# Attention and two MLPs on one Trainium2 core: weight jobs in three steps an f tile apart, and other points for loads on the SP queue

## The chip, the cores and the metric

The kernel runs on one core of one Trainium2 chip. The metric is the device time of one execution in microseconds (us). The engines are TensorE (PE in the profile, PEld for its weight loads), VectorE (DVE), ScalarE (ACT), GpSimd (POOL) and SyncE (SP, which here only issues DMAs). SP, ScalarE and POOL each have an instruction stream of their own from which they issue DMAs in order.

## The reference

```
scores = q k^T / sqrt(64)            # (4, 8, 576, 64): batch, heads, positions, head size
# heads 0..3 see the last 32 positions, heads 4..7 every 32nd position before and at their own
attn   = softmax(where(mask, scores, -1e9)) v
x      = attn with heads side by side          # 2304 tokens x 512
x      = (s * relu(x w_in)^2 + b) w_out        # w_in 512 x 2048, w_out 2048 x 512
out    = ((x w_a) * (x w_b)) w_o               # w_a, w_b 512 x 1536, w_o 1536 x 512
```

All data are float32; the weights arrive as 64-bit floats, and each is turned into a float32 on the chip by integer operations.

## The kernel before

**Numbers as two words.** Every matmul operand is a pair of words: a high one that ScalarE copies into the matmul's type, and a low one that VectorE gets by subtraction. A product is three passes (high x high, high x low, low x high).

**First MLP (`h_mm`, `o_mm`).** Tokens come in five groups n = 0..4 of 512, 384, 512, 384 and 512. For each n there are 16 tiles f. `h_mm` makes 12 matmuls, then ScalarE applies ReLU (L795) into the one buffer `r`, squares it and makes the high word; VectorE makes the low word `gt` (L123 or L806). `o_mm` comes two tiles behind and adds 12 matmuls to four accumulating banks `acc`. The attention of group n + 1 and the conversion of the second MLP's weights run beside the tiles of n = 1, 2 and 3.

**Conversion (`convert_w2`, class `Stream`).** In 37 steps the generator loads 64-bit words (`raw`, two buffers; w_a, w_b, w_o of a tile in turn, kinds 0, 1, 2), converts those of the step before, and stores them to DRAM as `w2d`. For kind 2 it also splits words and stores them as `w2o` (L858). `Stream` calls it at most once an f tile: `due` grows by a rate, and a step takes 1 plus what it yields; kind 2 yields `MORE`. The load of w_b goes into the buffer that the split of w_o leaves.

**Weight jobs (`sums`, `work`).** The second MLP uses Strassen-like sums of weight quarters: s1, s2, s3, s4 from the plain words a11, a12, a21, a22. A job loads two plain tiles `w2r` (POOL, L876), makes the four sums in a tile `w2t` (VectorE, L887; two buffers), copies the high word into a `spare` room (ScalarE, L894), subtracts for the low word (VectorE, L897), and stores both (POOL, L902) to `w2s` or `w2o`. These are eight calls of a generator: load, four sums, high, low, stores. 16 jobs run in n = 4: `work(f + 1)` at tile f calls the load of the next job, then all the rest of its own. Two more run in pair 0 of the second MLP.

**Second MLP.** It has three pairs of 384-token blocks. For each pair, 12 tiles g multiply seven weight forms with seven forms of x, in the order a11, s2, s3, s1, a12, a22, s4, six matmuls each (`product`, tile `pp`): banks pa, pb and pd of a pool of three, and pc of a pool of one, are taken anew at each g. `fill("s2", i)` and `fill("s3", i)` load forms from `w2s`; `source` loads plain words into `wsrc` and `fill("a11", i)`, `fill("a22", i)` split them on ScalarE and VectorE. Both engines' work is in an order written out by `act` and `dve` (each instruction behind the last), and SP's loads by `queue_sp`. At g = 5 `x2_load` loads the x of the next pair (1.5 MB), `x2_bias` and `x2_forms` turn it into forms later. Then 42 products `o2_mm` make the output; `o2_load` loads their weights `o2w` (256 KB) into NW rooms in turn. `o2_post` and `send` add banks up and store the output in pieces of 32 columns.

**What sets the order.** Where no order is written, the framework's scheduler fixes each engine's order when the kernel is built, with times that it simulates; `after` and `in_order` add edges. A tile that takes a buffer waits for the last user of it.

## Time and profile before

| | us |
|---|---|
| median of 3 runs | 916.59 (916.41 to 917.19) |
| the profiled execution | 914.19 |
| its span, first to last instruction | 912.5 |
| TensorE matmul busy in the span | 881.8 (97%) |
| TensorE weight load busy | 807.7 (89%) |
| VectorE busy | 681.7 (75%) |
| ScalarE busy | 408.2 (45%) |
| POOL busy | 143.0 (16%) |

Times in the rows are microseconds from the span's start. n = 4 begins near 395 us, the second MLP's pair 0 near 492, its output products near 590. An engine executes in order, so an instruction that waits holds up all behind it. "Granted clock" is the share of TensorE's full clock of 2.4 GHz; the lower level is 0.5.

### The profile page before, as it was taken

What the parts mean: (1) busy time and instruction counts of PE and PEld (TensorE: products, weight loads), DVE (VectorE), ACT (ScalarE), POOL (GpSimd) and SP (SyncE); (2) the same over time, 40 slices, a digit from 0 to 9 for tenths busy, and PEclk for the clock granted to TensorE, in tenths of its full rate; (3) what the DMA queues carried; (4) which work ended last, traced back from release to release, by engine and by line L of the source; (5) the groups of instructions that cost most, each with busy time, mean ns of one, the idle gap of its engine ahead of it and who ended that gap; (6) DMA issues with size and microseconds to landing.
All of it is one profiled execution on the core that took longest, in us unless ns stands there. A gap on an engine that the chain in (4) does not pass through costs nothing.

```text
span 912.5 us, 17335 instructions
## 1 busy us (share of the span) xinstructions
PE 881.8 (97%) x6274; PEld 807.7 (89%) x6274; DVE 681.7 (75%) x1411; ACT 408.2 (45%) x878; POOL 143.0 (16%) x289
## 2 busy tenths in 40 slices
PE   8999999999999989999999899999999999999996
PEld 6778889998888879997878889999989999999995
DVE  6898986776776867737667668896867896786883
ACT  6777764444433343456555224263224273232350
POOL 6000000000110011114443101007100005100013
PEclk9999999999999999999999999999999999999999
DMA  9966535775865767458988786787675787666585
GB/s 229 293 190 167 160 76 138 179 192 150 237 193 158 180 197 189 142 165 294 319 293 311 268 305 220 255 271 227 208 254 175 258 270 220 210 202 200 160 270 154
DMA packets 184260, 195.69 MB, mean 214 GB/s; under 512 B 107856, under 2 KB 137296, under 8 KB 184176
## 3 DMA queue, kind: packets, MB, share of 16 engines
q1 hardware_dynamic: 165760, 146.98, 54.9%
q0 software_dynamic: 15536, 46.90, 14.7%
q10 hardware_dynamic: 2880, 0.72, 0.4%
q8 instruction: 49, 0.80, 0.4%
q14 instruction: 35, 0.29, 0.1%
HBM read 152.08 MB, written 42.47 MB: 213 GB/s over the span
## 4 chain that ended last, share of the span: by engine, by line
PE 56%; DMA 13%; issue 13%; DVE 7%; ACT 5%; POOL 4%; SPq 2%; POOLq 0%; DVEq 0%; ACTq 0%
PE pp L99 24%; PE o L99 12%; PE h L99 8%; PE acc L99 7%; DMA wsrc<-w2d 3%; DMA w2d<-w2s 1%; DMA w2s<-w2t 1%; DMA raw<-in_moe_w_b_dram 1%; DMA o2w<-w2o 1%; POOL w2s L902 1%; DMA wf<-w2s 1%; SPq L284 1%; POOL w2r L876 1%; ACT raw L141 1%; PE po L99 1%
## 5 line engine op out<-in xcount | busy, mean ns | idle before, releaser
L99 PE MATMUL pp<-x2w,wf 128*128 128x384 f32 x1296 | 235.3, 338 | 8.1 <-DVE u L618 4.6
L99 PEld LDWEIGHTS pp<-x2w,wf 128*128 128x128 f32 x1296 | 228.1, 190 | 10.0 <-DVE u L618 5.2
L99 PE MATMUL h<-x,w 128*128 128x512 f32 (+1 forms) x960 | 219.0, 376 | 2.6 <-ACT r L795 2.2
L99 PE MATMUL acc<-gt,w 128*128 128x512 f32 (+2 forms) x960 | 211.4, 369 | 1.1 <-ACT w L122 1.0
L99 PEld LDWEIGHTS acc<-gt,w 128*128 128x128 f32 x960 | 175.9, 188 | 24.6 <-ACT w L122 1.4
L99 PEld LDWEIGHTS h<-x,w 128*128 128x128 f32 x960 | 172.6, 189 | 28.2 <-ACT r L795 3.3
L99 PE MATMUL o<-gf,o2w 128*128 128x384 f32 x756 | 133.4, 337 | 2.4 <-DMA o2w<-w2o 2.4
L99 PEld LDWEIGHTS o<-gf,o2w 128*128 128x128 f32 x756 | 131.3, 188 | 4.1 <-DMA o2w<-w2o 2.6
L613 ACT ACTIVATE gf<-quad 128x384 fp32r<-128x384 f32 x126 | 64.9, 524 | 94.3 <-DVE quad L618 64.9
L1276 POOL DMA_DIRECT2D out_dram<-ot x93 | 52.2, 570 | 295.9 <-DVE ot L1262 285.4
L795 ACT ACTIVATE r<-h 128x512 f32<-128x512 f32 (+1 forms) x80 | 44.4, 555 | 118.8 <-PE h L99 90.4
L618 DVE TENSOR_TENSOR gf<-quad,gf 128x384 fp32r<-128x384 f32 x126 | 67.5, 554 | 7.1 <-ACT gf L613 5.1
L618 DVE TENSOR_TENSOR quad<-pp,quad 128x384 f32<-128x384 f32 x108 | 59.8, 554 | 8.1 <-PE pp L99 6.5
L805 DVE TENSOR_TENSOR r<-r 128x384 f32<-128x384 f32 (+1 forms) x48 | 28.9, 603 | 40.9 <-ACT gt L802 40.8
L141 ACT ACTIVATE raw<-raw 128x512 f32<-128x512 f32 x66 | 42.9, 676 | 24.2 <-DMA raw<-in_moe_w_b_dram 19.2
L613 ACT ACTIVATE wf<-wsrc 128x512 fp32r<-128x512 f32 x36 | 22.6, 628 | 65.6 <-PE pp L99 44.1
L850 POOL DMA_DIRECT2D w2d<-w2s x36 | 19.7, 548 | 191.5 <-DVE w2s L157 160.9
L147 DVE SCALAR_TENSOR_TENSOR raw<-raw 128x512 uint32<-128x512 uint32 x66 | 44.4, 689 | 1.4 <-ACT raw L141 0.7
L99 PE MATMUL pp<-x2w,wh 128*128 128x384 f32 x216 | 43.5, 335 | 0.8 <-DVE quad L618 0.7
L613 ACT ACTIVATE quad<-pp 128x384 f32<-128x384 f32 x36 | 17.5, 486 | 54.6 <-PE pp L99 54.6
L618 DVE TENSOR_TENSOR quad<-quad 128x384 f32<-128x384 f32 x72 | 40.0, 555 | 1.3
L99 PEld LDWEIGHTS pp<-x2w,wh 128*128 128x128 f32 x216 | 37.9, 188 | 1.4 <-DVE quad L618 1.4
(171 smaller groups left out, 990.0 us busy)
## 6 DMA issues: line engine op xcount, KB each, us to landing
wf<-w2s SPq DMA_DIRECT2D x72, 512.0 KB
o2w<-w2o SPq DMA_DIRECT2D x126, 256.0 KB
raw<-in_moe_w_out_dram SPq DMA_DIRECT2D x28, 512.0 KB
w2d<-w2s POOLq DMA_DIRECT2D x36, 256.0 KB, 4.0
w2r<-w2d POOLq DMA_DIRECT2D x36, 256.0 KB, 4.6
wsrc<-w2d SPq DMA_DIRECT2D x36, 256.0 KB
raw<-in_moe_w_in_dram SPq DMA_DIRECT2D x16, 512.0 KB
raw<-in_moe_w_a_dram SPq DMA_DIRECT2D x12, 512.0 KB
```

The costliest lines, as they stand in the source:

```text
L99: last_pe[:] = [nc.tensor.matmul(*args, **kwargs).ins]
L141: nc.scalar.activation(out=high.bitcast(F32), in_=high.bitcast(F32), func=AF.Copy, scale=HIGH_SCALE)
L147: nc.vector.scalar_tensor_tensor(out=low, in0=high, scalar=3, in1=low, op0=ALU.logical_shift_left, op1=ALU.bitwise_or)
L284: nc.sync.dma_start(out=room[p0:p0 + STR, first_:first_ + (z - a) // STR], in_=at[e])
L613: i = nc.scalar.activation(**kwargs).ins
L618: i = getattr(nc.vector, method)(**kwargs).ins
L795: relu = nc.scalar.activation(out=r, in_=ph, func=AF.Relu)
L805: nc.vector.tensor_tensor(out=r, in0=r, in1=r, op=ALU.mult)
L850: nc.gpsimd.dma_start(out=w2d[i - 1], in_=w)
L876: nc.gpsimd.dma_start(out=t, in_=w2d[i])
L902: nc.gpsimd.dma_start(out=w2s[g][:, :, e] if own else w2o[g - NG2][:, 3 + i * m:3 + (i + 1) * m, e], in_=z.bitcast(F32).rearrange("p (i c) ...
L1276: engines[k % len(engines)].dma_start(out=at.rearrange("(j t) c -> t j c", t=STR), in_=st[i * STR:(i + 1) * STR, j:j + m].rearrange("t j a ...
```

## The change

- `MORE` grows from 0.35 to 0.45 and is yielded by kind 0; the split's store goes from POOL to SP.
- `work(j)` now calls job j's high copy, then the four sums of job j + 1, then job j's low word and stores, then the load of job j + 2. Before the loop, job 0's load and sums and job 1's load are called. The single `spare` room serves three jobs and not four.
- In n = 4 the fills and sources move to earlier tiles: s2 of 0 from f = 11 to 10, a11 of 0 from 12 to 11, the source of a11 of 1 from 13 to 11, s3 of 0 from 13 to 12, a11 of 1 from 15 to 13, s2 of 1 from 14 to 13. s3 of 1 moves from behind the loop to f = 14, and the source of a11 of 2 from f = 15 to behind the loop.
- The next pair's x is loaded two products later at g = 5, behind the source of a22.
- The s2 and s3 forms of the next pair's first two tiles are loaded at output products 16, 20, 24 and 28 instead of g = 10 and 11.
- Output weights get a seventh room (a new pool `wx`).
- The last stores of the output go over SP and ScalarE, no longer over POOL too.

```diff
-    MORE = 0.35
+    MORE = 0.45
@@ convert_w2
-                    nc.gpsimd.dma_start(
+                    nc.sync.dma_start(
                         out=w2o[f // 2][:, f % 2:f % 2 + n].rearrange("p i e c -> p (i e c)"),
...
-                yield MORE * (kind == 2)
+                yield MORE * (kind == 0)
@@ n = 4
-            rooms_s = lambda g: [spare if len(begun) < 5 else spare_s[next(spares)]]
+            rooms_s = lambda g: [spare if len(begun) < 4 else spare_s[next(spares)]]
...
+            def take(j, n):
+                if 0 <= j < EARLY:
+                    for _ in range(n):
+                        next(added[j])
             def work(j):
-                if j + 1 < EARLY:
-                    next(added[j + 1])
                 begun.append(j)
-                if j < EARLY:
-                    for _ in added[j]:
-                        pass
+                take(j, 1)
+                take(j + 1, 4)
+                take(j, 2)
+                take(j + 2, 1)
             with after(list(behind)):
-                work(0)
+                take(0, 4)
+                take(1, 1)
...
-                    work(f + 1)
+                    work(f)
...
-                if f == NG2 - 1:
+                if f == 10:
                     fill("s2", 0)
-                if f == NG2:
+                if f == 11:
                     fill("a11", 0)
-                if f == NG2 + 1:
                     source("a11", 1)
+                if f == 12:
                     fill("s3", 0)
-                if f == NG2 + 2:
+                if f == 13:
+                    fill("a11", 1)
                     fill("s2", 1)
-                if f == NG2 + 3:
-                    fill("a11", 1)
-                    source("a11", 2)
+                if f == 14:
+                    fill("s3", 1)
@@ second MLP
-    NW = 6
+    NW = 7
...
     source("a22", 1)
-    fill("s3", 1)
+    source("a11", 2)
...
@@ g == 5, ahead of product a11
-            if pair + 1 < NP2 and g == 5:
-                xr = in_order(x2_load, pair + 1)
-                later_x = [x2_bias(xr), x2_forms(xr)]
...
@@ g == 5, behind product s2
+            if pair + 1 < NP2 and g == 5:
+                xr = in_order(x2_load, pair + 1)
+                later_x = [x2_bias(xr), x2_forms(xr)]
...
-            in_order(fill, "s2", i + 2)
+            if g < NG2 - 2:
+                in_order(fill, "s2", i + 2)
...
-            in_order(fill, "s3", i + 2)
+            if g < NG2 - 2:
+                in_order(fill, "s3", i + 2)
...
-        engines = (nc.sync, nc.scalar, nc.gpsimd) if last else (nc.gpsimd,)
+        engines = (nc.sync, nc.scalar) if last else (nc.gpsimd,)
...
+                if i in (16, 20, 24, 28):
+                    in_order(fill, ("s2", "s3")[i // 4 % 2], (pair + 1) * NG2 + (i - 16) // 8)
```

## Rows read from the trace of the kernel before

**Rows 1.** TensorE's waits: instruction <- releaser: us in total, times, longest us
```profile
PE pp L99 <- DVE u L618: 4.6, 2, 2.5
PE pp L99 <- DMA wf<-w2s: 3.3, 1, 3.3
PE pss L99 <- DVE x L123: 3.1, 1, 3.1
...
PE o L99 <- DMA o2w<-w2o: 2.4, 4, 1.0
PE h L99 <- ACT r L795: 2.2, 2, 1.1
```

**Rows 2.** Windows: length, busy PE, PEld, DVE, ACT, POOL, granted clock, DMA share, GB/s
```profile
341.00:346.00 5.00, 5.00 (x49) 4.91 (x50) 3.92 (x10) 1.53 (x4) 0.54 (x1) 0.66 0.55 164
505.90:509.80 3.90, 3.90 (x14) 3.90 (x15) 1.40 (x4) 0.00 (x0) 0.00 (x0) 0.56 1.03 412
```

**Rows 3.** Timeline of SP where the first MLP ends: start, us, what
```profile
491.23 0.32 SPq L119 DMA_DIRECT2D wsrc<-w2d  x1
...
496.52 0.72 SPq L119 DMA_DIRECT2D wsrc<-w2d  x1
```

**Rows 4.** Chain of waits there: start, us, what
```profile
497.29 8.46 DMA wf<-w2s
```

**Rows 5.** Timelines of ScalarE and VectorE there, with [idle before <-releaser]
```profile
497.92 0.62 ACT L613 ACTIVATE wf<-wsrc 128x512 fp32r<-128x512 f32 x1
501.17 0.42 ACT L613 ACTIVATE wh<-wsrc 128x256 fp32r<-128x256 f32 x1 [2.63 <-DMA wsrc<-w2d]
...
498.69 0.68 DVE L618 TENSOR_TENSOR wf<-wsrc,wf 128x512 fp32r<-128x512 f32 x1
499.52 0.56 DVE L618 TENSOR_TENSOR quad<-pp,quad 128x384 f32<-128x384 f32 x1
```

**Rows 6.** Timeline of SP at g = 5 of pair 0
```profile
535.96 0.98 SPq L119 DMA_DIRECT2D xr<-o  x2
537.10 0.51 SPq L119 DMA_DIRECT2D wsrc<-w2d  x1
...
542.83 5.04 SPq L119 DMA_DIRECT2D wsrc<-w2d  x2
```

**Rows 7.** Timeline of VectorE behind it
```profile
547.10 0.43 DVE L618 TENSOR_TENSOR wh<-wsrc,wh 128x256 fp32r<-128x256 f32 x1 [4.48 <-ACT wh L613]
```

**Rows 8.** Windows in the output products of pair 0 and ahead of pair 1's
```profile
611.00:625.00 14.00, 14.00 (x83) 14.00 (x82) 13.96 (x29) 8.79 (x18) 6.54 (x12) 1.00 0.89 279
726.00:733.00 7.00, 6.37 (x37) 6.04 (x35) 6.24 (x13) 2.86 (x7) 0.00 (x0) 1.00 1.03 386
```

**Rows 9.** SP's timeline at pair 0's output; DMA issues (KB, us to landing)
```profile
590.89 5.45 SPq L119 DMA_DIRECT2D o2w<-w2o  x6
...
w2r<-w2d POOLq DMA_DIRECT2D x36, 256.0 KB, 4.6
```

**Rows 10.** VectorE's timeline in n = 4; tile w2t's DMAs
```profile
466.44 0.76 DVE L887 TENSOR_TENSOR w2t<-w2r 128x256 f32<-128x256 f32 x2 [2.31 <-DMA w2s<-w2t]
...
DMA to landing us min/median/max: 3.6/5.4/9.0
```

**Rows 11.** Timelines of POOL, SP and ScalarE in n = 3
```profile
329.40 0.54 POOL L858 DMA_DIRECT2D w2o<-raw  x1 [3.37 <-DVE raw L123]
...
334.16 0.39 SPq L129 DMA_DIRECT2D raw<-in_moe_w_b_dram  x1
...
338.98 0.68 ACT L141 ACTIVATE raw<-raw 128x512 f32<-128x512 f32 x1 [5.06 <-DMA raw<-in_moe_w_b_dram]
```

**Rows 12.** The chain's last pieces; DMA issues of the output
```profile
902.89 2.46 issue
905.35 0.65 POOLq L1465
...
out_dram<-ot POOLq DMA_DIRECT2D x5, 96.0 KB, 3.9
```

More of the change, by code (lines that the diff above doesn't have):

```diff
@@ L1189, in sparse_attention_two_mlps @@
     pool = lambda name, bufs: ctx.enter_context(tc.tile_pool(name=name, bufs=bufs, reuse_waits="tile"))
-    ws, tmp, rp, gq, rq = pool("ws", 2), pool("tmp", 6), pool("rp", 5), pool("gq", NQ2), pool("rq", 4)
+    ws, tmp, rp, gq, rq, wx = (
+        pool(*i) for i in (("ws", 2), ("tmp", 6), ("rp", 5), ("gq", NQ2), ("rq", 4), ("wx", 1))
+    )
     def add(out_, in0, in1, op=ALU.add):
@@ L1226, in o2_load @@
                 hp.tile([P, 2, HALF], F32R, tag="rw"[len(wrooms)], name="o2w") if len(wrooms) < 2
-                else p2.tile([P, 2, HALF], F32R, tag="r", name="o2w", bufs=4)
+                else p2.tile([P, 2, HALF], F32R, tag="r", name="o2w", bufs=4) if len(wrooms) < 6
+                else wx.tile([P, 2, HALF], F32R, tag="w", name="o2w")
             )
```

## The prediction

> **What bounds the kernel now.** I read the page's engine table first: TensorE's matmuls are busy 881.8 of 912.5 us, so the time is TensorE's own work plus about 31 us of holes, and a change that leaves the matmuls alone, as this one does, can only win or lose holes. Next come TensorE's waits, which name the holes [rows 1]: 4.6 us in two waits for a VectorE addition, 3.3 us in one wait for a weight load, 3.1 us for an attention split, 2.4 us for the second MLP's output weights, 2.2 us for ScalarE's ReLU. Then the windows behind the long holes [rows 2]: after the attention split's the mean granted clock is 0.66 over 5.0 us, after the weight load's 0.56 over 3.9 us, that is, part of the window runs at the lower of the two levels (1.2 instead of 2.4 GHz), and the loss is 5.0 x 0.34 = 1.7 and 3.9 x 0.44 = 1.7 us. The second of the additions' waits (pair 1) repeats the pattern, 1.7 us again; the first (2.5 us) and the one-microsecond waits don't. Last come the queues at each hole, which say what was late.
>
> The profiled execution took 914.19 us (span 912.5); the median of the three timed runs is 916.59, 2.4 us more. I add up gains against the profiled execution and take them from the median.
>
> **Part 1: where the first MLP ends.** The third hole is the load of the weight form s3 of the second f tile. It was issued behind all o1 stores and took 8.46 us to 505.75 [rows 4], so TensorE stood from 505.9 - 3.3 = 502.6 on. The change issues this load inside the first MLP (at f = 14) and gives its old place to the plain words a11 of the third f tile. Removed: 3.3 + 1.7 of clock = 5.0 us. But a11 of the third tile was issued at 491.23, ahead of the four o1 stores, and now goes behind them and behind a22, which was issued at 496.52 [rows 3]. That load adds a wait: ScalarE's conversion of a11 and VectorE's subtraction stand, in the written order of both engines, ahead of the addition that frees the PSUM bank of product s3 in the next tile. a22 landed at 501.17, when ScalarE could start on it [rows 5]: 4.65 us. a11 follows it on the queue with 256 KB; at the 279 GB/s of the second MLP's window [rows 8] that is 0.9 us more, so 502.1. Behind it come a ScalarE conversion of about 0.6, VectorE's 0.68 and the addition's 0.56 [rows 5]: bank free at 504.0, against 502.6. A hole of 1.4 us comes back; holes of about 1 us cost no clock. Net -3.6 us. Ends: if a11 lands with a22, 0.5 us come back (-4.5); if it takes the 8.46 us of the load whose place it has, it lands at 505.8, the hole is 5.1 us and the clock drops again (+1.8).
>
> **Part 2: the x load of the next pair.** The two additions' waits are the same event in pairs 0 and 1. At g = 5 the queue issued x (1.5 MB) at 535.96 and only then the 128 KB of a22, at 537.10 [rows 6]; ScalarE and VectorE could use a22 at 547.1, VectorE having stood 4.48 us in order [rows 7], and the addition behind it held the bank that TensorE wanted. The change puts the x load two products later in the written order, behind that a22. Removed: 4.6 us of holes and the 1.7 us of clock behind the second, 6.3 us. Late next is a11 of g = 8, issued at 542.83 [rows 6] behind x, s2 and s3. The bytes ahead of it are the same as before, and it is wanted about 4 us later than that a22 was: by my count of products near 549.8, while 1.3 MB of s2, s3 and a11 at 386 GB/s [rows 8] behind x (in by 546.6) land by 550.0 at the latest. I take 0.1 us in all: -6.2. If it were as late as a22 was (9.46 us, so 552.3), 2.5 us would come back in each pair, and the clock loss.
>
> **Part 3: output weights and S forms.** TensorE waits 2.4 us in four waits for output weights [rows 1]. The longest, 1.0 us, is in pair 0, and pair 1 has its like; two short ones of 0.2 us are at the end. In pair 0 the seventh weight was issued at 590.89 behind two 512 KB forms and one plain load. The change takes the forms of g = 10 and 11 out of this place, into the output loop at i = 16, 20, 24 and 28, and adds a seventh room, so that a weight is issued six products ahead of its use and not five; a product's rhythm is (5.45 - 0.32) / 5 = 1.03 us [rows 9]. Removed: 2.35 us. Added: 4 x 512 KB in 16.5 us = 126 GB/s upon 279 GB/s [rows 8], together 405. At the 386 GB/s that a stretch of this kernel has reached, the queue falls behind by 19 x 16.5 / 386 = 0.8 us; a 256 KB load takes 4.6 us to land on another queue [rows 9], and 5.4 is under 6.2, so TensorE waits for nothing. At the capacity that 279 GB/s at a share of 0.89 suggests (313), it falls behind by 4.9 us, and 9.5 - 6.2 = 3.3 us come back in pairs 0 and 1 each. I take 386, since it was seen. Of these loads the Trainium skill (DMA: Bandwidth & Descriptors, "Where 436 GB/s comes from") says that transfers between HBM and SBUF are limited to about 358 GB/s a core; the row of 386 already stands above that, and by the page 2.2 us of lag would give back an estimated 0.6 us a pair.
>
> **Part 4: the end.** The chain of waits closes on POOL, whose share in the last four stores is one, issued until 906.0; the span ends 6.5 us behind it [rows 12]. With the last stores on SP and ScalarE alone, POOL's last store is that at 902.9, and 6.5 us behind it is 909.4. SP's and ScalarE's stores, issued until about 906.0, land like others of their size in 3.9 us, by 909.9, with perhaps 0.8 us of closing work: 910.7 against 912.5, -1.8. Ends: 0, if the closing 6.5 us follow whatever is last, and -3.1.
>
> **Part 5: weight jobs.** The 16 jobs of the first MLP's last stage keep their instructions; sums, ScalarE copy and stores are spread over neighbouring f tiles. ScalarE need not stand for sums of the same tile any more. The added wait is VectorE's: a job's sums write one of two w2t buffers, and the store that must leave it was issued one tile ago, not two. Such a wait was 2.31 us long before 466.44, and these stores land in 3.6 to 9.0, in the middle 5.4 us [rows 10]. The tile's gt subtraction, on which the next ReLU waits, is queued behind. The existing ReLU waits cost 2.2 us in all [rows 1]. VectorE's order is not the written one even now (a job's subtraction stands among the next job's sums), so low subtractions may well precede the sums that must wait. Taken: 0, ends -2.2 and +15 (below).
>
> **Part 6: conversion.** The pause after each w_out step moves behind w_a and grows from 0.35 to 0.45 steps. Counted through, 31 of the 37 steps keep their tile; in n = 1 the steps b0, o0, b1, o1 and b2 come one tile later, in n = 3 a10 comes one earlier. The hole of 3.1 us (and 1.7 of clock) is at none of these. There a w_out split's store left POOL at 329.40, the load of w_b behind it left SP at 334.16, and ScalarE stood 5.06 us for it with an attention split queued behind [rows 11]. The store is now on SP: ahead of the attention loads it would come sooner, behind them (the queue is busy with them until about 331.7) later by some 2 us. Taken: 0, ends -4.8 and +4.8.
>
> **Sum:** -3.6 - 6.2 - 2.35 - 1.8 = -13.95: 914.19 to 900.2 profiled, 916.59 to **902.6 us**.
>
> **Rivals.** (a) VectorE's store waits: from the point where a tile's four sums stand ahead of its own low subtraction and the store has not landed, each tile does what the wait of 2.31 us did, about 1.1 us of hole [rows 1, 10]. In 14 tiles that is +15.1: 917.7, slower than before. For it: a store's 5.4 us against a tile of about 5.5 us. Against: gt has three buffers and ReLU a slack of one output product. Chance 0.10. (b) The boundary's hole stays, now for a11: +5.4, 908.0. For it: DMA engines are full there. Chance 0.15. (c) x only moves the wait on to a11: 2.5 + 2.5 + 1.7 = 6.7, 909.3. Chance 0.09. (d) The forms saturate the output loop: 6.6 back, 909.2. Chance 0.07. (e) The split's store comes later on SP and the conversion's hole grows or doubles: 907.4. Chance 0.10; that it vanishes: 897.8, chance 0.07.
>
> **How the numbers follow.** The forecast itself has 0.42. Two of (b) to (e) together end near 912 to 914. The range 898 to 912.5 leaves out (a), most of those pairs and the best case's tail, about 0.2. A measurement here can tell 0.2% (1.8 us). Faster by more than that: all but (a) and some pairs, 0.84; within 0.2%: 0.05; slower: 0.11.
>
> **What would show it.** Right: no wait for a form near 502.6 but a short one behind VectorE; no wait in front of g = 6 of pairs 0 and 1, and one clock loss less there; no output-weight wait of 1 us; the span closing under 5 us after the last matmul's store is issued. Wrong: VectorE waits for w2s stores adding up to more than the present 8 us or so with ReLU waits behind them (a), ScalarE standing for plain words longer than now (b, c), output-weight waits past i = 20 (d), and a longer wait of SP for the split's stores (e).

## The result

| | before | after |
|---|---|---|
| median of 5 runs, us | 917.14 (916.41 to 917.69) | 922.14 (920.60 to 923.80) |
| profiled execution, us | 914.19 | 923.55 |
| its span, us | 912.5 | 921.8 |

The ratio is 1.0059 with a 95% interval of 1.0043 to 1.0075: half a per cent slower, where 902.6 us had been forecast (range 898 to 912.5).

TensorE's waits in the profile after (the page's view: who waited, for whom, us in total, times, longest); they answer to [rows 1]:

```profile
PE h L99 <- ACT r L795: 8.5, 6, 2.9
PE pp L99 <- DVE v L618: 3.0, 1, 3.0
...
PE ppt L102 <- DVE lpt L450: 2.2, 1, 2.2
PE po L99 <- ACT pT L488: 2.1, 1, 2.1
PE pss L99 <- DVE x L123: 1.9, 1, 1.9
PE pp L99 <- DVE quad L618: 1.3, 2, 1.1
PE o L99 <- DMA o2w<-w2o: 1.3, 3, 0.6
PE po L99 <- DVE sqk L436: 1.2, 1, 1.2
```

All the waits that the change aimed at are smaller or gone: the two for the addition `u` (4.6 us), the one for a form `wf` (3.3 us), half of those for output weights. In their place stand waits for ScalarE's ReLU (2.2 before, 8.5 now), for the addition `v`, and three for the attention (`ppt`, `po`).

Where the span went is seen when the same matmul is found in both traces (TensorE's timeline). Each row is the time from the first matmul of a stage to the first of the next, in the one profiled execution of each kernel:

| stage | before | after | difference | predicted |
|---|---|---|---|---|
| n = 1 to 3 (134 us to the start of n = 4) | 262.9 | 276.0 | +13.1 | 0 |
| n = 4, up to g = 0 of pair 0 | 94.9 | 100.8 | +5.9 | 0 |
| g = 0 to 3 of pair 0 (up to the first matmul of g = 3) | 27.9 | 28.1 | +0.2 | -3.6 |
| rest of pair 0's tiles | 69.6 | 66.1 | -3.5 | -2.5 |
| output products of pair 0 | 45.1 | 45.6 | +0.5 | -1.0 |
| pair 1's tiles | 91.2 | 87.4 | -3.8 | -3.7 |
| output products of pair 1 | 45.1 | 45.2 | +0.1 | -1.0 |
| pair 2 | 132.9 | 132.0 | -0.9 | -0.4 |
| last matmul to the end | 8.6 | 6.4 | -2.2 | -1.8 |

Windows of the profile (from:to, length, busy time of TensorE, its weight loads, VectorE, ScalarE and POOL, granted clock, DMA share, GB/s), first those of before for the first two of these rows, then those of after for the first four:

```profile
134.30:397.20 262.90, 259.39 (x2692) 231.62 (x2688) 185.37 (x433) 106.19 (x243) 30.05 (x54) 0.99 0.64 176
397.20:492.10 94.90, 92.61 (x413) 76.03 (x410) 61.40 (x114) 56.98 (x95) 36.02 (x57) 1.00 0.83 282
```

```profile
134.20:410.20 276.00, 265.11 (x2690) 236.15 (x2688) 184.07 (x433) 105.61 (x243) 23.30 (x42) 0.98 0.60 167
410.20:511.00 100.80, 94.59 (x413) 77.15 (x410) 62.70 (x118) 56.50 (x96) 36.54 (x58) 0.98 0.80 277
511.00:539.10 28.10, 24.01 (x128) 23.38 (x127) 17.74 (x36) 7.89 (x17) 3.68 (x7) 0.94 0.78 265
539.10:605.20 66.10, 65.89 (x380) 65.46 (x379) 53.43 (x106) 24.00 (x51) 5.64 (x8) 1.00 0.75 247
```

In the first window after, TensorE stood for 10.9 us (276.00 less 265.11; 3.5 before), and at a granted clock of 0.98 some of its work ran at the lower level; the fourth window has no hole of note. The x load did what it was to do. The loss is in the two stages of the first MLP that the prediction put at nothing.

### The profile page after: what moved, and what is told of

It is laid out like the page before. It is cut to its first block, busy times and chain, and to the rows that moved or that the text cites. A ratio compares the mean times of both kernels' runs of the same rounds, so it can differ in the third digit from the quotient of the medians.

```text
span 921.8 us, 17308 instructions
## 1 busy us (share of the span) xinstructions
PE 887.0 (96%) x6274; PEld 811.3 (88%) x6274; DVE 680.0 (74%) x1411; ACT 406.5 (44%) x878; POOL 135.2 (15%) x276
## 4 chain that ended last, share of the span: by engine, by line
PE 70%; DMA 10%; issue 9%; ACT 4%; DVE 4%; POOL 2%; SPq 1%; POOLq 0%; ACTq 0%; DVEq 0%
PE pp L99 27%; PE h L99 13%; PE o L99 13%; PE acc L99 11%; DMA o2w<-w2o 2%; PE po L99 1%; DMA w2s<-w2t 1%; DMA w2d<-w2s 1%; DMA w2r<-w2d 1%; DMA raw<-in_moe_w_a_dram 1%; DMA o<-o1s 1%; PE pss L99 1%; SPq L284 1%; PE fpo L99 1%; PE ppt L102 1%
## 5 line engine op out<-in xcount | busy, mean ns | idle before, releaser
L99 PE MATMUL pp<-x2w,wf 128*128 128x384 f32 x1296 | 232.9, 336 | 1.3 <-DVE quad L618 1.3
L99 PE MATMUL h<-x,w 128*128 128x512 f32 (+1 forms) x960 | 224.4, 383 | 8.5 <-ACT r L795 8.5
L99 PEld LDWEIGHTS h<-x,w 128*128 128x128 f32 x960 | 176.7, 193 | 35.5 <-ACT r L795 10.6
L141 ACT ACTIVATE raw<-raw 128x512 f32<-128x512 f32 x66 | 42.8, 673 | 31.1 <-DMA raw<-in_moe_w_a_dram 16.4
```

The lines of the kernel that those rows point to most:

```text
L99: last_pe[:] = [nc.tensor.matmul(*args, **kwargs).ins]
L141: nc.scalar.activation(out=high.bitcast(F32), in_=high.bitcast(F32), func=AF.Copy, scale=HIGH_SCALE)
```

## The experiments

"Before" beside each result is the kernel before, measured on the same chip at the same time. Executions of one kernel differ by 5 us and more (the kernel before took 912.0 to 923.8), so beside the median I give the stage that the experiment is about, from the one execution whose trace was kept. A stage that is not edited can swing from kernel to kernel as well: with the conversion as before, n = 4 starts anywhere from 394.3 to 398.7.

### The conversion: which half, which step

**Conversion undone.** The changed kernel with the pause and the split's store as before:

```diff
-    MORE = 0.45
+    MORE = 0.35
...
-                    nc.sync.dma_start(
+                    nc.gpsimd.dma_start(
                         out=w2o[f // 2][:, f % 2:f % 2 + n].rearrange("p i e c -> p (i e c)"),
...
-                yield MORE * (kind == 0)
+                yield MORE * (kind == 2)
```

> The changed kernel with the conversion as it was before (pause 0.35 behind w_out, split's store on POOL). By the two traces, TensorE's first tile of n = 4 starts 13.0 us later in the changed kernel, all of it lost in n = 1 to 3. Theory 1 (the conversion alone costs this, stages add up): 922.1 - 13.0 = 909 us, n = 4 starting near 397 us. Rival (the scheduler's order differs everywhere, the loss is not the conversion's): above 915 us.

Measured: 908.04 us, before 915.93 (ratio 0.9915, 0.9886 to 0.9943); n = 4 starts at 397.0, where it did before (397.2; 410.2 with the change). The conversion is the 13 us, and what is left of the change is a gain of 8 us. The window over the same stages:

```profile
134.00:397.00 263.00, 258.79 (x2693) 230.14 (x2688) 185.53 (x433) 105.85 (x243) 29.77 (x54) 1.00 0.63 176
```

Against the window after, TensorE stands 6.7 us less (263.00 less 258.79 is 4.2), and the same matmuls take 6.3 us less (258.79 against 265.11), at a granted clock of 1.00 and not 0.98. So about half of the 13 us is matmuls that ran slower.

**Store alone undone, pause alone undone.** One half of the diff above each.

> The changed kernel with only the split's store back on POOL, the pause left behind w_a. Theory S (the store makes SP stand for VectorE and holds up the loads behind it): 10 to 13 us are gained, 909 to 912 us. Theory P (the moved pause puts w_b, w_out and w_a one tile apart where there were two): under 3 us are gained, 919 to 922 us.

> The changed kernel with only the pause back (0.35, behind w_out), the split's store left on SP. Theory S: under 3 us are gained, 919 to 922 us. Theory P: 10 to 13 us are gained, 909 to 912 us.

Measured: with the store back on POOL (the new pause left) 917.41 (ratio 1.0022, 1.0002 to 1.0043), n = 4 from 404.7; with the old pause (the store left on SP) 909.36 (0.9936, 0.9909 to 0.9964), n = 4 from 400.6. By the start of n = 4 the pause alone costs 7.5 us, the store alone 3.4, both together 13. By the medians, against the 908.0 of the kernel with neither, it is 9.4, 1.3 and 14.1; the profiled execution with the store alone (912.37) was the slowest of its eight, so its 3.4 may be too high. Which load is late tells the two apart. ScalarE's waits ahead of the first step of a conversion (L141), before, then with the new pause alone, then with the store on SP alone, and SP's waits ahead of that store in the last of these:

```profile
ACT raw L141 <- DMA raw<-in_moe_w_a_dram: 3.9, 3, 1.8
```

```profile
ACT raw L141 <- DMA raw<-in_moe_w_a_dram: 13.1, 5, 6.4
```

```profile
ACT raw L141 <- DMA raw<-in_moe_w_a_dram: 3.9, 2, 2.4
```

```profile
SPq L858 <- DVE raw L123: 13.1, 4, 6.3
SPq L858 <- DVE sm L447: 2.7, 2, 1.5
```

The new pause makes 13.1 us out of 3.9. The store on SP doesn't touch these waits, but it makes SP stand for VectorE's split, 16 us in these two rows. That this holds up the loads behind it is not seen in ScalarE: its waits for all three weights at L141 add up to 24.1 us before and 20.6 with the store on SP alone.

**The place of the pause.** Is it that the pause is longer, or that it stands behind w_a?

```diff
-    MORE = 0.45
+    MORE = 0.35
...
-                    nc.sync.dma_start(
+                    nc.gpsimd.dma_start(
...
                 yield MORE * (kind == 0)
```

> The changed kernel with the split's store back on POOL and the pause back at 0.35 steps, but still behind w_a. Against the kernel before, the steps b0, o0, b1, o1 and b2 come one f tile later in n = 1 and o11 one later in n = 3; w_a's step a10 is where it was. Theory 'place': what costs time is that the conversions of b2, o2 and a3 now stand in three f tiles in a row; then the third stage (n = 4) starts near 404.7 us, as with the longer pause, and the median is 914 to 918. Theory 'length': the longer pause does it; then n = 4 starts near 397 and the median is 907 to 910, as with the whole conversion undone.

Measured: 914.02 us, before 916.55 (0.9983, 0.9956 to 1.0011), n = 4 from 402.9. The place costs some 6 us: 5.9 by this start (against 397.0), 6.0 by the medians.

**One step of it moved back.** By counting `due` through, this place puts b0, o0, b1, o1 and b2 one f tile later in n = 1 (the letter is the weight, the number its tile). First b2 alone goes back:

```diff
-                yield MORE * (kind == 0)
+                yield MORE * (kind == (2 if f == 2 else 0))
```

> The kernel with the pause behind w_a at its old length and the store on POOL (914.0 us), and the pause of the third f tile alone back behind w_out. Against it only one step moves: b2 is at f = 11 of n = 1 again, so that b2, o2 and a3 no longer stand in three f tiles in a row; b0, o0, b1, o1 stay one tile later than before. Theory: that row of three is what holds w_a's load and makes the holes at 193 to 219 us: n = 4 starts at 397 to 398 (402.9 without), the median is 907 to 910. Rival: the later b0 to o1 have used up the slack already: n = 4 above 401, 912 to 915.

Measured: 915.75 (0.9987, 0.9966 to 1.0008), n = 4 from 405.0. My theory fell: taking the three conversions apart gained nothing. The timelines of the kernel before this one (the pause behind w_a, old length) said what else it could be. First SP, then ScalarE; start, us, what, and in brackets the idle time before it and what ended it:

```profile
183.15 2.43 SPq L529 DMA_DIRECT2D sv<-in_v_dram  x6
185.68 1.79 SPq L284 DMA_DIRECT2D qk<-in_q_dram  x4
187.58 1.50 SPq L129 DMA_DIRECT2D raw<-in_moe_w_a_dram  x1
...
192.89 0.66 ACT L141 ACTIVATE raw<-raw 128x512 f32<-128x512 f32 x1 [6.13 <-DMA raw<-in_moe_w_a_dram]
193.45 0.51 ACT L802 ACTIVATE gt<-r 128x384 fp32r<-128x384 f32 x1
...
194.47 0.37 ACT L488 ACTIVATE pT<-ppt 128x256 f32<-128x256 f32 x1
```

SP's timeline of the kernel before, at the same load:

```profile
180.91 0.53 SPq L129 DMA_DIRECT2D raw<-in_moe_w_a_dram  x1
```

The load of a2 is issued by the step that converts o1. That step is one tile later, so the load has gone behind ten attention loads (`sv`, `qk`) and starts at 187.58 instead of 180.91. The step that converts a2 has not moved. ScalarE stands 6.1 us for it, and the copy for `gt` and the attention's `pT` queue behind; TensorE waits 1.2 us for `pT`, then 1.2 for an addition of VectorE's (`sqk`), and from 190 to 224 us the granted clock is 0.95. So the next kernel moves o1 back.

```diff
-                yield MORE * (kind == 0)
+                yield MORE * (kind == (2 if f == 1 else 0))
```

> The kernel with the pause behind w_a at its old length and the store on POOL (914.0 us), and the pause of the second f tile alone back behind w_out: b1 and o1 are in their old f tiles (7 and 8 of n = 1), b0 and o0 stay one later, and b2, o2 and a3 stay in three tiles in a row. Theory 'lead': the load of w_a is issued in the step of the w_out before it; the pause used to stand between the two, now it stands behind w_a, so w_a's load has one f tile less ahead of its conversion. With o1 one tile later the load of a2 went behind ten attention loads on SP's queue (187.58 instead of 180.91), and ScalarE stood 6.1 us for it with an attention copy and a copy of gt queued behind. With o1 back it is issued near 181, the holes at 193 to 219 go, n = 4 starts at 397 to 399, the median is 907 to 910. Rival: any conversion step one tile later does it, whichever: n = 4 stays above 401, 912 to 915.

Measured: 909.80 us, before 917.17 (0.9913, 0.9882 to 0.9944), n = 4 from 398.6. The same two lines in this kernel:

```profile
183.83 0.53 SPq L129 DMA_DIRECT2D raw<-in_moe_w_a_dram  x1
184.41 2.27 SPq L529 DMA_DIRECT2D sv<-in_v_dram  x6
...
188.01 0.67 ACT L141 ACTIVATE raw<-raw 128x512 f32<-128x512 f32 x1
```

The load stands ahead of these `sv` loads again and ScalarE doesn't wait. So this one load is 4.3 of the 5.9 us.

The three stages apart (us from first matmul to first matmul, by the same traces) show it better than the start of n = 4:

| kernel | n = 1 | n = 2 | n = 3 |
|---|---|---|---|
| before | 80.0 | 97.7 | 85.2 |
| with the change | 86.4 | 102.4 | 87.2 |
| conversion undone | 80.0 | 98.7 | 84.2 |
| new pause alone | 85.9 | 98.1 | 86.3 |
| store on SP alone | 81.2 | 101.6 | 83.6 |
| pause behind w_a, old length | 85.3 | 97.9 | 85.5 |
| the same, b2 back | 88.1 | 97.6 | 84.9 |
| the same, o1 back | 80.3 | 98.7 | 85.0 |

In the twelve kernels here with the old conversion, n = 1 takes 80.0 us in each, n = 2 from 97.6 to 98.8, n = 3 from 82.3 to 85.2. So the place of the pause costs 5.3 us in n = 1, and 5.0 of them go with o1 moved back. The store on SP costs 3 to 4 us in n = 2, where TensorE stands 1.9 us for a ReLU and runs slower behind it (store on SP alone):

```profile
247.00:256.00 9.00, 7.08 (x25) 5.41 (x24) 7.08 (x19) 2.27 (x5) 0.54 (x1) 0.82 0.76 179
```

What made that ReLU late was not tested.

### n = 4: VectorE's waits for stores

**A third room for the words of the weight jobs.** In the changed kernel VectorE stands 5.0 us for a store in n = 4. Timelines of POOL, VectorE and ScalarE:

```profile
461.14 0.76 POOL L902 DMA_DIRECT2D w2o<-w2t  x1 [1.64 <-DVE w2t L897]
...
467.62 0.76 DVE L887 TENSOR_TENSOR w2t<-w2r 128x256 f32<-128x256 f32 x2 [5.03 <-DMA w2o<-w2t]
...
469.77 0.69 DVE L123 TENSOR_TENSOR gt<-r,gt 128x512 fp32r<-128x512 f32 x1
...
470.55 0.60 ACT L795 ACTIVATE r<-h 128x512 f32<-128x512 f32 x1 [5.67 <-DVE gt L123]
```

This is the mechanism of rival (a). A third room lets the sums write words whose store was issued a tile earlier. The room is a part of x that n = 4 no longer reads:

```diff
-        t = p2.tile([P, 4, HALF], F32, tag="s", name="w2t", bufs=2)
+        turn.append(g)
+        if third and len(turn) % 3 == 0 and len(turn) < EARLY - 1:
+            t = third[0].bitcast(F32).rearrange("p (i c) -> p i c", i=4)
+        else:
+            t = p2.tile([P, 4, HALF], F32, tag="s", name="w2t", bufs=2)
...
-                        room = xp[1].tile([P, 4 * DM], F32R, tag="x", name="spare")
+                        room = xp[1].tile([P, 6 * DM], F32R, tag="x", name="spare")
+                        third.append(room[:, 4 * DM:])
```

> The changed kernel with a third room for the words of the weight jobs (w2t) in the first MLP's last stage, so that a job's sums overwrite words whose stores were issued one tile earlier than now. Theory: the 5 us wait of VectorE for a store, with the subtraction of gt behind it, makes the 2.9 us hole near 468 and its clock loss and some of the one microsecond holes; the stage n = 4 falls from 100.8 us to 95 to 96.5, the median from 922 to 917. Rival: other waits (ScalarE's copies, the rooms of the high words) hold the same stage: above 99 us, 920 to 922.

Measured: 916.58 us, before 916.55 (0.9996, 0.9972 to 1.0021), and n = 4 takes 94.8 us, before's 94.9. VectorE's waits for a job's stores, before, with the change and then with the third room, and the window of n = 4 in the last:

```profile
DVE w2t L887 <- DMA w2s<-w2t: 8.5, 5, 2.9
DVE w2t L887 <- DMA w2o<-w2t: 2.3, 2, 1.8
```

```profile
DVE w2t L887 <- DMA w2o<-w2t: 6.6, 2, 5.0
DVE w2t L887 <- DMA w2s<-w2t: 5.7, 4, 3.2
```

```profile
DVE w2t L892 <- DMA w2s<-w2t: 1.5, 2, 1.4
```

```profile
408.40:503.20 94.80, 93.28 (x413) 75.81 (x411) 63.41 (x119) 57.51 (x96) 36.49 (x58) 1.00 0.86 298
```

With the third room the 6 us are gone. The sum of these waits says little: 10.8 us before and 1.5 with the third room go with the same stage length, 12.3 with the change. What differs is the longest: 2.9 before, 5.0 now, and 3.3 with the conversion undone, where the stage takes 96.8. Behind the wait of 5.0 stand a ReLU, TensorE's hole of 2.9 us and the only stretch at the lower clock in this stage:

```profile
471.00:476.00 5.00, 4.80 (x14) 3.87 (x15) 4.08 (x8) 2.71 (x6) 2.46 (x4) 0.66 0.78 265
```

**What brings them.** The old order of the jobs, once with the new conversion and once with the old one:

```diff
+                if j + 1 < EARLY:
+                    next(added[j + 1])
                 begun.append(j)
-                take(j, 1)
-                take(j + 1, 4)
-                take(j, 2)
-                take(j + 2, 1)
+                if j < EARLY:
+                    for _ in added[j]:
+                        pass
...
-                take(0, 4)
-                take(1, 1)
+                work(0)
...
-                    work(f)
+                    work(f + 1)
```

> The changed kernel with the weight jobs as before (load of the next, then the whole job in one tile). In the changed kernel n = 4 takes 5.9 us more from its first tile to the second MLP. Theory J (the three-step jobs cost that): 922.1 - 5.9 = 916 us. Rival F (the earlier fills and sources in n = 4 put ScalarE and VectorE work among the ReLUs and cost it): 921 to 923 us.

> The changed kernel with both the conversion and the weight jobs as before (908.0 us with the conversion alone undone); the forms and plain words at f = 8 to 14 stay where the change put them. What is left open is which part brings VectorE's store waits into n = 4, which a third room takes away. Theory 'jobs': the new order of the jobs does; n = 4 goes back to 94.5 to 95.5 us (96.8 with the conversion alone undone), the median is 905 to 907. Theory 'forms': the form loads at f = 10 to 14 share the DMA engines with the jobs' stores and make them late, whichever order the jobs have; n = 4 stays at 96.5 to 99.5 us, the median is 908 to 911.

Measured: 921.94 (1.0052, 1.0025 to 1.0080) with n = 4 at 99.7 us, and 904.23, before 916.88 (0.9864, 0.9827 to 0.9902), with n = 4 at 98.6 us. So the jobs' order does not bring the waits by itself: they are there with the old one too, and what these kernels still have of the change in n = 4 is the form and plain-word loads moved to f = 10 to 14. With these loads where they were, and the jobs as before (the kernel with the x load alone, below), n = 4 is 94.9. With the old order, then, the moved loads bring 3.7 to 4.8 us. By the medians, with the conversion as before, the new order may still cost some 4 us (908.0 against 904.2, measured apart, with ratio intervals that overlap); the stage lengths (96.8 against 98.6) say the opposite. With the moved loads, two rooms and the new order the stage ran from 96.8 to 103.0 us in ten kernels, and the two with the old order lie inside that: an effect of the order is not shown, and the order without the moved loads was not run. With three rooms the stage ran from 93.4 to 94.8 in six kernels.

### The boundary of the MLPs

Between g = 0 and g = 3 the s3 wait went, and two waits came, both in the tile g = 1. Timelines of POOL and VectorE after:

```profile
516.01 0.56 POOL L876 DMA_DIRECT2D w2r<-w2d  x1 [1.93 <-DMA o<-o1s]
...
517.13 1.80 POOL L876 DMA_DIRECT2D w2r<-w2d  x3
...
520.46 0.69 DVE L618 TENSOR_TENSOR wf<-wsrc,wf 128x512 fp32r<-128x512 f32 x1 [4.29 <-ACT wf L613]
...
526.28 0.42 DVE L618 TENSOR_TENSOR w2t<-w2r 128x256 f32<-128x256 f32 x1 [3.86 <-DMA w2r<-w2d]
526.62 0.55 DVE L618 TENSOR_TENSOR u<-pp,u 128x384 f32<-128x384 f32 x1
```

The first is a11 of the third tile behind the o1 stores (1.1 us of hole). The second is the sum of a weight job of pair 0: its plain words, issued by POOL from 516 on, are there only at 526, and the addition that frees TensorE's bank stands behind it (3.0 us and a lower clock behind).

The length of this stretch swings too. In the ten kernels that have the change's loads here and the late jobs as they were, it runs from 25.0 to 28.6 us, and the wait for `v` is there in five of them (1.4 to 3.0 us) and absent in five. A difference of up to 3 us in it shows nothing by itself.

**The late job's sums a tile later; a11 early again.** Both on the kernel with the conversion undone (908.0), which has the two holes at 1.75 and 2.3 us:

```diff
-        for at in ((g if j == 0 else 2, 1), *((g + 1, k) for k in (1, 2, 3, 4)), (g + 2, 5), (g + 2, 6), ...
+        d = 1 if j == 0 else 0
+        for at in (
+            (g if j == 0 else 2, 1), *((g + 1 + d, k + d) for k in (1, 2, 3, 4)),
+            (g + 2 + d, 5), (g + 2 + d, 6), ...
```

> The changed kernel with the conversion wholly as before (908.0 us), and the sums and copies of the first late weight job one f tile later in the second MLP's first pair. Theory: the hole of 2.3 us at the second tile and the 1.7 us of clock behind it are VectorE standing for that job's plain words, landed 11 us after their issue; one tile (8 us) later they are there, and the median is 904. Rival: the loads of the weight forms are as late as the job's words, so TensorE stands for them or for VectorE somewhere else in the first four tiles: 907 to 909.

```diff
+                if f == 15:
+                    source("a11", 2)
...
     source("a22", 1)
-    source("a11", 2)
```

> The changed kernel with the conversion wholly as before (908.0 us), and the plain words a11 of the third tile issued at f = 15 again, ahead of the four o1 stores; s3 of the second tile stays at f = 14. Theory: the hole of 1.75 us ahead of product s3 of the second tile is ScalarE waiting for a11 behind those stores; it goes, and the median is 906.3. Rival: the late job's words behind it are what VectorE waits for anyway, and what is won here is added to the next hole: 907.5 to 908.5.

Measured: sums later, 909.54 (0.9920, 0.9893 to 0.9948), g = 0 to 3 29.4 us: the wait for `v` went and the one for `quad` grew from 1.75 to 4.8, since ScalarE had a11 only after 6.67 us of waiting. a11 early, 910.38 (0.9928, 0.9904 to 0.9952): the `quad` hole went, that for `v` grew to 2.9; and n = 4 took 103.0 us. Both rivals held in kind: what one hole gives, the other takes. That points at a third thing for which both wait, the DMA engines; these two runs do not show it. In the kernel with the conversion undone they are nearly full there:

```profile
494.00:500.00 6.00, 6.00 (x36) 6.00 (x36) 4.83 (x8) 2.62 (x4) 2.02 (x5) 1.00 1.02 361
500.00:505.00 5.00, 3.39 (x20) 3.06 (x18) 1.08 (x2) 1.31 (x3) 1.57 (x3) 1.00 0.97 308
```

**The late words out of the way.** POOL issues the 1 MB of the late jobs as soon as a room is free. Now they go over SP's queue, at g = 3 and g = 7:

```diff
-    def sums(g, room, vector, scalar):
+    def sums(g, room, vector, scalar, load=nc.gpsimd.dma_start):
...
-            nc.gpsimd.dma_start(out=t, in_=w2d[i])
+            load(out=t, in_=w2d[i])
...
-    added = [sums(g, lambda g: ring_row, partial(dve, "tensor_tensor"), act) ...
+    added = [sums(g, lambda g: ring_row, partial(dve, "tensor_tensor"), act, queue_sp) ...
...
+        g += 3
-        for at in ((g if j == 0 else 2, 1), *((g + 1, k) for k in (1, 2, 3, 4)), ...
+        for at in ((g, 1), *((g + 1, k) for k in (1, 2, 3, 4)), ...
```

> The changed kernel with the conversion wholly as before (908.0 us), and the plain words of the two late weight jobs (1 MB) loaded in the written order of SP's queue at g = 3 and g = 7 of the first pair, not by POOL as soon as a room is free; their sums, copies and stores follow as far behind them as now. Theory: both holes of the first two tiles (1.75 and 2.3 us, and 1.7 of clock) are DMA time: the 1 MB takes an estimated 2.7 us at 386 GB/s in the stretch where a11 of the third tile and the forms are wanted; both go, g0 to g3 falls from 28.1 to about 23, the median to 902 to 904. Rival: the o1 stores ahead of a11 on SP's queue set the first hole, and it stays at about 1.5 us: 904 to 906. Second rival: the loads of the late words on SP's queue delay the forms behind them at g = 4 and 8: 907 or more.

> The kernel with the late words on SP's queue, and the third room for the words of the weight jobs in the first MLP's last stage as well. Theory: the third room takes the store waits of VectorE away here too, the stage n = 4 falls to 94.8 us (before's) whatever it is in the kernel without: 900 to 903 in all. Rival: without the added store waits the jobs run earlier, their stores fill the DMA engines ahead of the boundary, and the boundary's holes come back: 904 to 907.

Measured: 910.05 us (0.9925, 0.9898 to 0.9953), and with the third room 903.51 (0.9866, 0.9836 to 0.9895). g = 0 to 3 falls from 28.1 to 25.8 and 25.6: the `v` hole is gone in both, the `quad` hole stays at 2.1 and 1.8, as the first rival said; 25.6 still lies within the swing above. The rest of pair 0 grows from 66.2 to 68.8: a wait of 1 us in the tile g = 7 and three short ones, at a granted clock of 1.00. In all, the median without the third room is no better than the 908.0 without this move, as the second rival had it (907 or more). The third room has n = 4 at 94.7 us, against 98.0 without.

**All of it, a11 early.** The kernel with late words on SP, the third room and the forms spread (next section), and a11 at f = 15:

> The kernel with the conversion as before, the late words on SP's queue, the third room and the forms spread (900.9 us), and the plain words a11 of the third tile issued at f = 15 again, ahead of the o1 stores. Theory: that place is the whole of the hole of 1.6 us ahead of product s3 of the second tile; with n = 4 steady by the third room the hole goes and nothing comes back: 898.5 to 899.5. Rival: with a11 early the o1 stores and the forms behind come later and another wait of the first tiles takes its place: 900.5 to 902.

Measured: 900.34 us, before 917.39 (0.9811, 0.9793 to 0.9829). TensorE has no hole in the first three tiles, 21.9 us instead of 23.8 with the forms spread:

```profile
492.10:514.00 21.90, 21.90 (x127) 21.86 (x127) 15.69 (x30) 7.01 (x15) 1.35 (x2) 1.00 0.78 256
```

The two kernels built on this one (below) have 21.9 as well. So a11's late place is worth 1.9 us there (3.7 against the 25.6 above), and only once the late words were out of the way.

### The x load alone

The kernel before, with the x load behind the product of s2 and nothing else changed:

```diff
-            if pair + 1 < NP2 and g == 5:
-                xr = in_order(x2_load, pair + 1)
-                later_x = [x2_bias(xr), x2_forms(xr)]
...
+            if pair + 1 < NP2 and g == 5:
+                xr = in_order(x2_load, pair + 1)
+                later_x = [x2_bias(xr), x2_forms(xr)]
             if g == NG2 - 1:
```

> The kernel before with the x load alone moved behind the next product. Theory: the two waits of TensorE for a VectorE addition at g = 6 of pairs 0 and 1 go and nothing else changes: -6.3 to -7.3 us, 909 to 910. Rival: part of the gain measured in the changed kernel comes from the forms moved out of the pair's end, so the load alone gives less: 911 to 914.

Measured: 908.26 us, before 916.98 (0.9919, 0.9890 to 0.9947). Pair 0 behind g = 3 falls from 69.6 to 66.0, pair 1 from 91.2 to 87.9: 6.9 us. The theory held for these two stages; the span falls by 6.0, the median by 8.7. Two stages that the edit doesn't touch moved as well: n = 3 is 2.2 us shorter (its attention hole was 1.1 us and not 3.1), and g = 0 to 3 is 2.4 longer. TensorE's waits of that kernel show what the latter is:

```profile
PE pp L99 <- DVE v L618: 3.7, 1, 3.7
...
PE pp L99 <- DMA wf<-w2s: 1.7, 1, 1.7
```

The s3 form came earlier this time (1.7 us for the 3.3 of before), and the wait for the late job's words, until now under that hole, came out at 3.7 us.

### The output loop and the late jobs' place

**Forms spread over the output loop:**

```diff
-                if i in (16, 20, 24, 28):
-                    in_order(fill, ("s2", "s3")[i // 4 % 2], (pair + 1) * NG2 + (i - 16) // 8)
+                if i in (8, 16, 24, 32):
+                    in_order(fill, ("s3", "s2")[i // 8 % 2], (pair + 1) * NG2 + (i - 8) // 16)
```

> The kernel with the late words on SP's queue and the third room, and the four forms of the next pair in the output loop at i = 8, 16, 24 and 32, not 16, 20, 24 and 28. Theory: at 16 to 28 weights and forms and stores together ask for what the engines move at most there (406 GB/s), the queue falls behind and TensorE waits at i = 32 (0.6 and 1.2 us); spread over twice the products it doesn't: 1 to 1.8 us less than the kernel without it, 899 to 901. Rival: the waits are single late packets and come anywhere: within 0.7 us of the kernel without it.

Measured: 900.94 us against 903.51 (before 916.98; 0.9841, 0.9809 to 0.9873). The median moved as the theory had it, its reason did not: the output products of pairs 0 and 1 take 45.8 and 45.6 us against 45.4 and 46.1, and TensorE's waits for output weights don't fall. First without, then with the forms spread:

```profile
PE o L99 <- DMA o2w<-w2o: 2.2, 4, 0.9
```

```profile
PE o L99 <- DMA o2w<-w2o: 2.9, 5, 1.0
```

The 2.6 us lie in n = 3 (1.1) and at the boundary (1.8), which this edit doesn't touch. I take it for no effect.

**The late jobs otherwise placed.** Both loads ahead of x (g = 2 and 4), then the first job wholly ahead of x, its stores too, and the second behind it (loads at g = 2 and 8):

```diff
-        g += 3
-        for at in ((g, 1), *((g + 1, k) for k in (1, 2, 3, 4)), ...
+        g = (3, 6)[j]
+        for at in (((2, 4)[j], 1), *((g, k) for k in (1, 2, 3, 4)), ...
```

```diff
+        g = (3, 9)[j]
+        for at in (((2, 1), (8, 4))[j], *((g, k) for k in (1, 2, 3, 4, 5, 6)), (g + 1, 1), (g + 1, 2), (g + 1, 3)):
```

> The same with a11 early, and the two late jobs' words loaded at g = 2 and g = 4, both ahead of the x load of g = 5 on SP's queue, not at 3 and 7. Theory: the wait of 1.1 us at g = 8 (and the clock behind it) is a11 of that tile behind x and the second job's words; it goes, pair 0 from g = 3 falls from 68.4 to about 66.2 us: 2.2 us less than the kernel without, 896 to 897.5. Rival: the wait is x's own (it was weighed as such), and stays: within 0.7 us of the kernel without.

> The fastest kernel so far (a11 early, third room, forms spread: 900.3 us), with the first late job wholly ahead of the x load of g = 5 (load at g = 2, its 1 MB of stores at g = 4, not 6) and the second behind it (load at g = 8, stores at g = 10). Theory: the wait of 1.0 us at g = 8 is the sum of x, the first job's stores and the second job's load in two tiles; apart they fit, pair 0 from g = 3 falls from 68.3 to 66.2 us: 898 to 899. Rival: the late jobs collide with the forms wherever they are put: 900 to 901.

Measured: 900.38 (0.9824, 0.9797 to 0.9851) and 899.71 us (0.9807, 0.9769 to 0.9845). Pair 0 behind g = 3 takes 68.8 and 67.6 us, against 68.3 with loads at 3 and 7 and 66.2 with the words in POOL's hands. In the first the wait moved from g = 7 to three short ones at g = 6; in the second the longest left is one of 0.4 us, at g = 4. Neither theory held in size, and there was no clock to win back: it is 1.00 in this stretch with and without the wait. On SP's queue the late jobs cost pair 0 1.4 to 2.6 us wherever they were put. The last of these kernels has the lowest median of all, 1.9% below the kernel before; the three with a11 early (899.7 to 900.4) can't be told apart.

## Why the prediction was wrong

**Part 6, conversion (0 predicted, +13 measured).** This is the step that failed. The count of the steps was right: b0 to b2 come a tile later in n = 1. What was drawn from it was not: "The hole of 3.1 us (and 1.7 of clock) is at none of these", so nothing was charged. I had asked whether the moved steps touch the hole that there was, not what the moved steps issue. A step issues the next weight's load before it converts its own, and the load of a2 went with step o1 past ten attention loads, while its user stayed. 4 to 5 of the 13 us are shown to be this one load (n = 1 goes from 85.3 to 80.3 without its delay); about 6 come with the place of the pause, 7.5 to 9.4 with the pause. The store's move was rival (e), at a chance of 0.10 and a price of 4.8; alone it costs 1.3 us by the median and 3.4 by the stages, and together with the pause the two cost 2.1 to 3.4 more than their sum. That it comes through SP's wait for VectorE (16 us in the rows above) is argued: no run took that wait away by itself, and ScalarE's waits for weights did not grow with it.

**Part 5, weight jobs (0 predicted, ends -2.2 and +15; +5.9 measured).** The mechanism was named, as rival (a) at 0.10, and with the third room the whole loss goes. The size was off: four ReLU holes of 0.8 to 2.9 us, where before had two of 1.1, and one clock loss, not 14 tiles. The sign given for it, waits for `w2s` stores above 8 us, was not the right one: those fell from 8.5 to 5.7, and the long wait was for a `w2o` store. The reason was off too: with the old order of the jobs the stage is 3.7 to 4.8 us longer all the same, so the loads moved in beside the stores are enough, and part 1 did not charge its own move with that.

**Part 1, boundary (-3.6 predicted, +0.2 measured).** The s3 hole went (5.0), and a11 brought 1.1 us for the 1.4 worked out. What failed is the search for what is late next. Behind the s3 hole the late job's words were already late: VectorE's waits before have the row

```profile
DVE w2t L618 <- DMA w2r<-w2d: 5.9, 1, 5.9
```

which TensorE didn't feel, since the s3 hole lay over it. That wait came out as a hole of 3.0 us, and the window of 28.1 us has the clock of 0.94 again that it had before (0.06 x 28.1 = 1.7 us): 4.7 of the 5.0 us went back. I had listed VectorE's waits ahead of the hole and not those under it. How much goes back is partly luck: in the ten kernels with the same edit here the stretch came out between 3.0 us shorter and 0.7 longer than before.

**Part 2, x load (-6.2 predicted, -7.3 in the changed kernel, -6.9 alone).** Right, by the mechanism named: no wait ahead of g = 6, and the a11 of g = 8 was in time.

**Part 3, output weights (-2.35 predicted, about 0 measured).** The 1 us waits of pairs 0 and 1 went, and waits of 0.5 us near i = 32, behind the last form, came, with 0.3 for the issue in each. The term mis-sized is the lag of 0.8 us, and not by its capacity: 386 GB/s, which [rows 8] has from the first 7 us of pair 1's output loop, was reached in the changed kernel too, but late. The loop of pair 0 after, first where the forms begin, then around the wait near i = 32:

```profile
626.00:630.00 4.00, 4.00 (x25) 4.00 (x24) 4.00 (x9) 3.05 (x8) 0.00 (x0) 1.00 0.91 317
634.00:645.00 11.00, 10.46 (x58) 9.47 (x57) 9.38 (x20) 3.76 (x8) 6.59 (x13) 1.00 1.03 390
```

The sum took 386 over all 16.5 us; what kept the engines below it in the first half is not shown. By the page of the Trainium skill (DMA: Bandwidth & Descriptors, "Where 436 GB/s comes from") an estimated 0.6 us a pair was to come back, near what came; but its limit of about 358 GB/s was passed here, by the 390 of the second row.

**Part 4, the end (-1.8 predicted, -2.2 measured).** Right; nothing follows the last stores of SP and ScalarE:

```profile
916.59 0.85 SPq L1284 DMA_DIRECT2D out_dram<-ot  x2
916.59 0.91 ACTq L1284 DMA_DIRECT2D out_dram<-ot  x2
```

**The sum.** 13.1 + 5.9 are the two parts put at nothing; without them the span would have come out at 902.8 us, 9.7 below before's. Parts 1 and 3 gave some 6 less than predicted, parts 2 and 4 1.5 more. The rivals (a) and (e) were right in kind, but each stood alone at 0.10; that both could come, and a loss from both halves of the conversion's edit, was not priced. By the rivals' own prices two of (b) to (e) end at 912.8 to 915.9, not at 912 to 914.

## What to carry to other kernels

A generator's step that is moved carries the DMA issues inside it past other issues on the queue; cost each of them against the use that does not move. Before a hole is counted as gain, list what the other engines wait for underneath it: a wait that a hole covers comes out when the hole goes. Where a stage's length swings from kernel to kernel without being edited, look for a two-buffer store wait in it; one more room steadied n = 4 here. And where stages swing, compare each stage over several kernels before giving one of them a cause.

## What the runs showed of the hardware

- A 256 KB load of `w2r` that lands in 4.2 us in the median (the profile's DMA issues after) took 6.1 to 10.2 us at the boundary (four loads issued from 516.0 on, 9.3 in the middle), where o1 stores, job stores and forms were under way.
- The share of busy DMA engines and the bytes moved don't rise in step: in one output loop 0.91 at 317 GB/s and, 4 us later, 1.03 at 390.
- Holes of 1 to 2.2 us in n = 1 to 3 came with as much again in slower matmuls: 6.7 us of standing and 6.3 us of longer matmul time in the first window after, against the kernel with the conversion undone. It is not so for every hole: that kernel has one of 2.35 us at 341 us, and its clock is 1.00 over the whole window.
